# A new layout of the first stage: softmax passes of the first batch on VectorE, eight rooms for gated h, other slots for exp, slabs, w_out and loads

## The chip, the cores and the metric

The kernel runs on one core of one Trainium2 chip. The metric is the device time of one execution in microseconds, the median of three runs. All times below are microseconds unless marked ns. Engines are named as the profile names them: PE is TensorE's matmul stream and PEld its weight loads, DVE is VectorE, ACT is ScalarE, POOL is GpSimd, SP is SyncE, whose one queue issues every DMA of this kernel in program order.

## The reference, cut to what matters

Eight batches of eight heads with 576 tokens and head size 64 are reduced to 32 memory slots each, and the result goes through two gated feed-forward layers of 4608 tokens, width 512 and inner width 2048. The weights are handed in as 64-bit floats.

```python
a = exp(phi - phi.max(2)); a = a / (a.sum(2) + 1e-9)           # over tokens
k_m = einsum('bhsm,bhsd->bhmd', a, k)
v_m = einsum('bhsm,bhsd->bhmd', a, v)
s = (q @ k_m.T) / sqrt(64); s = exp(s - s.max(-1))
x = (s / (s.sum(-1) + 1e-9)) @ v_m                              # -> 4608 x 512
x = moe(x, w_in, w_out);  x = moe2(x, w_in2, w_out2)
# moe:  h = x @ w_in; g = h * sigmoid(1.702 h); g @ w_out
# moe2: the same with sigmoid(h)
```

## The kernel before, in words

**Stages.** Stage 1 (0 to about 380) is the attention of all batches and the first layer's w_in, up to the gated h, which goes to DRAM in `gs`. Stages 2, 3 and 4 (380 to 748, to 1110, to 1473) are the three other weight products; the change leaves their body alone and touches only the first few steps of stage 2. Every float32 product is made of three passes with a high and a low part of each operand, so each operand is rounded (a copy on ACT) and its rest is formed (a subtraction on DVE or POOL).

**Slots of stage 1.** A loop over 256 slots (L1003), 32 for each batch, sets the order. A slot is six matmuls of 128x288 (`first1`, L331) into one of four PSUM buffers `h`, and the gate, which ACT writes to `g` (L348, Silu). While exponentials are due nearby (the list `exps`, L827), the gate is a Tanh on ACT (L345) and one instruction on DVE (L346), which saves loads of ACT's function table. Two slots (two token halves `hf`) fill one `g` tile; there are five rooms for `g` (L342). `g_store` (L350) sends the tile to DRAM.

Ahead of its own gate a slot emits the operations that are listed for it with "e" (mostly evacuations and vector work), then come its matmuls and gate, then "p" (other matmuls), "l" (more evacuations), "d" (DMA issues). The table `PLAN` (L728) gives the slot of each operation for batch 1, for 2 and for 3 and later, counted from the start of the batch ahead. The first batch's order is written out in `start`, with the rest of it in `zero`.

**Attention of a batch.** phi is loaded, its maximum folded (`pm`, two halves on DVE, L172), subtracted, exponentiated (`phi_exp`, L201) and its sum folded (`es`, eight instructions on POOL, L175). `kv_mm` (L211, 72 matmuls) gives k_m and v_m. q is loaded in eight pieces, transposed on PE (`q_t`, L244) and copied out as `qT` (`q_e`, L248); `scores` (L256), a transposition on DVE (`soft_t`), maximum, subtraction (`soft_sub`, L282), exp (`soft_exp`, L286), sum, multiplication (`soft_mul`, L296), back transposition (`soft_back`, L300) and high and low part of the result (`soft_hi` L304, `soft3`) follow for each half. `wp_mm` multiplies v_m into w_in and gives a `slab` (ACT high L322, DVE low L326), four of them per batch; the slots' matmuls read slabs and attention output.

**Weights.** A 64-bit weight tile is converted in two ACT passes (L94, L95), a shift and a sign on DVE (L100, L105) and an addition on POOL (L111). The 16 tiles of w_in are converted in the first 25 slots. w_out is loaded in four groups of four tiles (`wo_load`, L394) through two rooms `raw` (L391), so that each load waits until the tile two before it is converted. Sums of these (`w_sums`) and their high and low parts (`w_high` L448, `w_low`) are spread over stage 1.

**Start of stage 2.** `r_fetch` (L495) reads `gs` back from slots given by `rf`, `a_prep` makes the operand tiles `op` (ACT L520, DVE L523); two of them are made in stage 1 at `mk`.

## Time and profile before

| | us |
|---|---|
| median of three runs | 1475.28 (1474.56 to 1476.45) |
| the profiled execution | 1474.05 |
| its span in the trace | 1472.3 |
| PE busy | 1396.1 (95%) |
| DVE busy | 963.1 (65%) |
| ACT busy | 812.2 (55%) |
| POOL busy | 207.0 (14%) |

The execution's own time holds 1.75 us outside the span; it lies 1.23 us under the median. PE is the engine with the most work in each stage. The page's rows by instruction group and the chain of waits show where it stood still; the windows by stage show in which part of the span.

### The profile page before, as it was taken

How to read it: one execution, taken by the hardware profiler on the slowest of the kernel's cores; microseconds unless marked ns; L12 is line 12 of the kernel's file. 1: busy time of each engine (PE TensorE's matmuls, PEld its weight loads, DVE VectorE, ACT ScalarE, POOL GpSimd, SP SyncE). 2: the span in 40 equal slices, each digit the busy share in tenths (PEclk: the TensorE clock that was granted, in tenths of full speed). 3: DMA queues.
4: the chain of work that ended last, by engine and by line, in shares of the span. 5: the costliest groups of instructions: out<-in, count | busy, mean ns of one | idle time of the engine just before them, and what ended most of it. 6: DMA issues, size and time to landing. Idle time of an engine off the chain costs nothing.

```text
span 1472.3 us, 27420 instructions
## 1 busy us (share of the span) xinstructions
PE 1396.1 (95%) x10776; PEld 1326.8 (90%) x10776; DVE 963.1 (65%) x1299; ACT 812.2 (55%) x1429; POOL 207.0 (14%) x193
## 2 busy tenths in 40 slices
PE   4789889999899999999999999999998999999998
PEld 3568677878899999999999999999998999999998
DVE  5745554544597898788877353454577776777765
ACT  3756766667455454455467565665674444444443
POOL 3423635432101111110000010111000000000000
PEclk9999999999999999999999999999999999999999
DMA  9777777945744836627234556465564524515320
GB/s 307 211 226 220 246 252 221 288 158 199 268 135 148 279 103 209 214 100 260 94 129 166 186 182 216 153 217 189 172 213 145 204 81 146 194 44 183 131 96 33
DMA packets 195296, 265.51 MB, mean 180 GB/s; under 512 B 50528, under 2 KB 158048, under 8 KB 195168
## 3 DMA queue, kind: packets, MB, share of 16 engines
q1 hardware_dynamic: 195168, 263.77, 53.9%
q8 instruction: 84, 1.38, 0.4%
q14 instruction: 44, 0.36, 0.1%
HBM read 159.91 MB, written 102.76 MB: 178 GB/s over the span
## 4 chain that ended last, share of the span: by engine, by line
PE 78%; DMA 7%; DVE 5%; ACT 3%; issue 1%; SPq 1%; POOL 0%; ACTq 0%; DVEq 0%
PE p L687 23%; PE p L537 17%; PE xb L625 13%; PE h L339 11%; PE y L625 10%; PE aa L256 2%; DMA xs<-o 1%; DMA rr<-gs 1%; DVE op L65 1%; PE a L211 1%; DMA q<-in_q_dram 1%; SPq L495 1%; DMA gs<-g 1%; PE a L244 1%; DVE r L62 1%
## 5 line engine op out<-in xcount | busy, mean ns | idle before, releaser
L537 PE MATMUL p<-op,wq 128*128 128x384 f32 x2016 | 358.4, 339 | 9.9 <-DVE op L65 4.5
L537 PEld LDWEIGHTS p<-op,wq 128*128 128x128 f32 x2016 | 353.0, 189 | 15.0 <-DVE op L65 7.7
L687 PE MATMUL p<-wq,op 128*128 128x256 f32 x3024 | 360.0, 282 | 4.2 <-ACT gq L635 2.5
L687 PEld LDWEIGHTS p<-wq,op 128*128 128x128 f32 x3024 | 359.6, 191 | 4.7 <-ACT gq L635 2.8
L520 ACT CAST op<-rr 128x768 fp32r<-128x768 f32 x216 | 179.2, 835 | 181.2 <-PE p L687 77.3
L339 PE MATMUL h<-attnT,slab 128*128 128x288 f32 x1536 | 239.2, 307 | 18.3 <-ACT g L348 14.0
L65 DVE TENSOR_TENSOR op<-rr,op 128x768 fp32r<-128x768 f32 x216 | 209.0, 974 | 66.2 <-ACT op L520 65.5
L339 PEld LDWEIGHTS h<-attnT,slab 128*128 128x128 f32 x1536 | 212.9, 193 | 41.6 <-ACT g L348 20.5
L625 PE MATMUL xb<-xq,wq 128*128 128x384 f32 x1152 | 216.4, 336 | 1.3 <-ACT e L665 0.9
L625 PEld LDWEIGHTS xb<-xq,wq 128*128 128x128 f32 x1152 | 201.4, 188 | 2.0 <-ACT e L665 1.2
L65 DVE TENSOR_TENSOR op<-r,op 128x768 fp32r<-128x768 f32 x120 | 123.2, 1031 | 73.8 <-ACT op L520 73.7
L625 PE MATMUL y<-xq,wq 128*128 128x384 f32 x864 | 166.6, 337 | 2.1 <-ACT e L675 1.0
L520 ACT CAST op<-r 128x768 fp32r<-128x768 f32 x120 | 99.4, 834 | 101.3 <-PE p L687 43.9
L625 PEld LDWEIGHTS y<-xq,wq 128*128 128x128 f32 x864 | 151.7, 188 | 3.0 <-ACT e L675 1.3
L348 ACT ACTIVATE g<-h 128x288 f32<-128x288 f32 x247 | 98.2, 420 | 77.2 <-PE h L339 59.4
L111 POOL TENSOR_TENSOR wst<-wst 128x512 int32<-128x512 int32 x24 | 40.9, 1704 | 488.4 <-DVE wst L105 279.5
L635 ACT ACTIVATE gq<-e 128x384 f32<-128x384 f32 x144 | 75.9, 527 | 28.7 <-DVE e L62 27.9
L62 DVE TENSOR_TENSOR e<-e,y 128x384 f32<-128x384 f32 x96 | 52.7, 552 | 47.4 <-PE y L625 45.5
L62 DVE TENSOR_TENSOR e<-e,xb 128x384 f32<-128x384 f32 x48 | 26.5, 553 | 84.0 <-PE xb L625 53.3
L65 DVE TENSOR_TENSOR slab<-aa,slab 128x512 fp32r<-128x512 f32 x62 | 39.8, 680 | 45.1 <-ACT slab L322 42.8
L448 ACT CAST wq<-wst 128x512 fp32r<-128x512 f32 x83 | 51.2, 620 | 25.1 <-DVE wst L65 15.0
L65 DVE TENSOR_TENSOR wq<-wst,wq 128x512 fp32r<-128x512 f32 x63 | 43.0, 687 | 13.4 <-ACT wq L448 13.3
(121 smaller groups left out, 1239.5 us busy)
## 6 DMA issues: line engine op xcount, KB each, us to landing
rr<-gs SPq DMA_DIRECT2D x120, 384.0 KB, 6.4
gs<-g SPq DMA_DIRECT2D x128, 288.0 KB, 4.0
gs<-gq SPq DMA_DIRECT2D x192, 192.0 KB, 1.9
r<-gs SPq DMA_DIRECT2D x72, 384.0 KB, 5.7
xs<-o SPq DMA_DIRECT2D x24, 384.0 KB, 3.6
xr<-xs SPq DMA_DIRECT2D x24, 384.0 KB, 4.4
out_dram<-o SPq DMA_DIRECT2D x24, 384.0 KB, 2.8
rawe<-in_moe_w_in_dram SPq DMA_DIRECT2D x16, 512.0 KB, 6.8
```

The lines of the kernel that those rows point to most:

```text
L62: eng.tensor_tensor(out=out, in0=a, in1=b, op=ALU.add)
L65: eng.tensor_tensor(out=out, in0=a, in1=b, op=ALU.subtract)
L111: nc.gpsimd.tensor_tensor(out=z, in0=z, in1=parts(t, dst)[0], op=ALU.add)
L256: nc.tensor.matmul(out=out[s][32 * j:32 * j + 32, 0:n], lhsT=st["kvT", b][r, i, 32 * j:32 * j + 32], rhs=rhs[j][r], start=True, stop=True)
L339: nc.tensor.matmul(out=h, lhsT=slab[b, f // 4, g][:, wi, f0:f0 + 128], rhs=x[:, g, xi], start=(g == 0 and n == 0), stop=(g == 1 and n == 2))
L348: nc.scalar.activation(out=t, in_=h, func=ACTF.Silu, scale=2.0)
L448: nc.scalar.copy(out=t[:, :, 0], in_=wst[m, c, k])
L520: nc.scalar.copy(out=t[:, :, 0], in_=s)
L537: nc.tensor.matmul(out=out[:, d, :HB], lhsT=w[:, s, wi, d * 128:(d + 1) * 128], rhs=t[:, s, gi], start=(start and p == 0 and s == 0 and n ...
L625: nc.tensor.matmul(out=out, lhsT=w[:, s, wi, f0:f0 + 128], rhs=x[:, s, xi], start=(start and s == 0 and n == 0), stop=(s == 1 and n == 2), ...
L635: nc.scalar.activation(out=t, in_=h, func=ACTF.Silu, scale=2.0)
L687: nc.tensor.matmul(out=out[:, d], lhsT=t[:, u, gi, d * 128:(d + 1) * 128], rhs=w[:, u, wi], start=(start and d != 1 and p == 0 and u == 0 ...
```

## The change

- `g` has eight rooms for five.
- `raw` is gone. The loads of the first three groups of w_out use two rooms of the pool that w_in's loads had used (`wo14`, `wo15`), in turn; the fourth group has one tile in the room of `kv`, with a place for each of its four loads.
- `es` can be folded on DVE in one instruction; it is so for batches 1 and 2, and on POOL for the later ones, at slot -7 for -14.
- In the first batch's softmax the multiplication of the first half and the subtraction of the second go from POOL to DVE. In the other batches `se` says which of the four subtractions and multiplications run on POOL (1 and -1) and which on DVE (0, -2): over the whole stage subtractions on POOL go from 4 to 9 and on DVE from 12 to 7.
- `qv` lets a copy of `qT` run on DVE (DVE 4 to 11 copies). `le` names the engine of the attention's low part (DVE 2 to 7, POOL 14 to 9). Some low parts and sums of w_out go to DVE (POOL 20 to 11 low parts).
- `ld` writes out the order of the first batch's loads, w_in and q mixed.
- The table has other slots in nearly every row. The exponentials' stretches begin one slot earlier in six batches; the list of them goes from (47,48), (79,80), ..., (175,176) to (46,48), (78,80), ..., (174,176). Gates by Tanh go from 9 to 14, Silu from 247 to 242; ACT loads its table 18 times in either.
- `rf` goes from [19, 20, 21, 22, 23, 2] to [20, 15, 22, 20, 27, 1], `mk` from [26, 29] to [21, 28]: the operand made first now stands one slot behind the issue of the fetch that it reads.

```diff
-            gt[b, f] = moe.tile([128, 2, HS], F32, tag="g", name="g", bufs=5)
+            gt[b, f] = moe.tile([128, 2, HS], F32, tag="g", name="g", bufs=8)
...
-            n = slice(2 * n, 2 * n + 2)
+            n = slice(2 * n, 2 * n + 2) if name == "pm" else slice(0, 4)
...
-    def raw():
-        return moe.tile([128, 512, 2], I32, tag="raw", name="raw", bufs=2)
...
-        st["wo", c, k] = wload(w1o, rows(f), cols(0), raw())
+        if c < 3:
+            t = wo_p.tile([128, 512, 2], I32, tag=f"wo{14 + k % 2}", name="raw")
+        else:
+            if k == 0:
+                t = att.tile([128, 2, 4, C9, D], F32, tag="kv", name="raw")
+                st["raw"] = t.rearrange("p a b c d -> p (a b c d)").bitcast(I32)
+            t = st["raw"][:, 1024 * k:1024 * k + 1024].rearrange("p (f w) -> p f w", w=2)
+        st["wo", c, k] = wload(w1o, rows(f), cols(0), t)
...
-                 'se': [0, 1, -2, 1]},
+                 'se': [1, 1, 0, 1],
+                 'ee': 1,
+                 'qv': [0, 0, 0, 0, 0, 0, 0, 1],
+                 'le': [0, 1]},
...
-             'wo': [[[53, 56, 62, 64], [62, 64, 65, 72], 73], [[101, 100, 105, 109], [108, 110, 114, 117], 121],
-                    [[151, 150, 157, 160], [156, 159, 165, 167], 173], [[216, 218, 222, 225], [222, 224, 227, 230], -3]],
+             'wo': [[[52, 54, 60, 61], [59, 61, 64, 69], 74], [[103, 97, 106, 109], [108, 109, 114, 117], 122],
+                    [[148, 147, 154, 157], [153, 156, 162, 166], 176], [[222, 224, 230, 232], [228, 231, 233, 236], 1]],
...
-        at(z + x["es"], "e", phi_fold, b, "es", ALU.add, nc.gpsimd)
+        at(z + x["es"], "e", phi_fold, b, "es", ALU.add, (nc.vector, nc.gpsimd)[x["ee"]])
...
-                at(z + y[9], "e", soft3, b, hf)
+                at(z + y[9], "e", soft3, b, hf, (nc.vector, nc.gpsimd)[x["le"][hf]])
```

On DVE, in the first batch's softmax (`sm` and `nat` are the sums and the scores of a half, `attnT` the low part of the result), the difference between the two orders is this:

```order
-L300 STREAM_TRANSPOSE at<-nat 128x576
-L274 STREAM_TRANSPOSE nat<-aa 128x288 x2
-L278 TENSOR_REDUCE mx<-nat 128x18
+L248 COPY qT<-a 128x288
+L296 TENSOR_TENSOR nat<-nat,sm 128x576
+L300 STREAM_TRANSPOSE at<-nat 128x576
+L274 STREAM_TRANSPOSE nat<-aa 128x288 x2
 L65 TENSOR_TENSOR attnT<-at,attnT 128x2x288
+L278 TENSOR_REDUCE mx<-nat 128x18
+L282 TENSOR_TENSOR nat<-nat,mx 128x576
```

The multiplication (L296) stands ahead of the back transposition and the subtraction (L282) ahead of what follows; both were on POOL, and one more copy of `qT` stands in front.

On ACT, ahead of the k_m and v_m matmuls of batch 2, where the second half of batch 1's scores is exponentiated and `qT` of batch 2 is copied; before:

```order
L286 ACTIVATE nat<-nat 128x576
L322 CAST slab<-aa 128x512 x2
L248 COPY qT<-a 128x288
L348 ACT_TABLE_LOAD
L348 ACTIVATE g<-h 128x288
L248 COPY qT<-a 128x288
```

and now:

```order
L201 ACTIVATE phi<-phi 128x576 x2
L345 ACTIVATE g<-h 128x288
L286 ACTIVATE nat<-nat 128x576
L248 COPY qT<-a 128x288 x2
L348 ACT_TABLE_LOAD
L348 ACTIVATE g<-h 128x288
L322 CAST slab<-aa 128x512
```

Both copies of `qT` now stand straight behind the exponential; the slab's two casts and the table load stand behind them.

On ACT, in the stretch of exponentials of batch 2's scores and batch 3's phi; before:

```order
L286 ACT_TABLE_LOAD
L286 ACTIVATE nat<-nat 128x576
L201 ACTIVATE phi<-phi 128x576
L345 ACTIVATE g<-h 128x288
L286 ACTIVATE nat<-nat 128x576
L201 ACTIVATE phi<-phi 128x576
L348 ACT_TABLE_LOAD
```

and now (L452 is a rounding of w_out, L448 in the numbering of before):

```order
L201 ACT_TABLE_LOAD
L201 ACTIVATE phi<-phi 128x576
L345 ACTIVATE g<-h 128x288
L286 ACTIVATE nat<-nat 128x576
L452 CAST wq<-wst 128x2x256
L345 ACTIVATE g<-h 128x288
L286 ACTIVATE nat<-nat 128x576
L201 ACTIVATE phi<-phi 128x576
L348 ACT_TABLE_LOAD
```

The same four exponentials and two table loads now hold two gates instead of one, and a rounding of w_out stands among them.

On POOL, around the additions that end the conversion of the first four w_out tiles (L111; `es` is batch 3's fold, `attnT` the low part of a result); before:

```order
L175 TENSOR_TENSOR es<-phi 128x128
L175 TENSOR_TENSOR es<-es,phi 128x128 x7
L65 TENSOR_TENSOR attnT<-at,attnT 128x2x288 x2
L111 TENSOR_TENSOR wst<-wst,raw 128x2x256 x4
L65 TENSOR_TENSOR wst<-wst 128x512 x2
```

and now:

```order
L175 TENSOR_TENSOR es<-phi 128x128
L175 TENSOR_TENSOR es<-es,phi 128x128 x7
L65 TENSOR_TENSOR attnT<-at,attnT 128x2x288
L111 TENSOR_TENSOR wst<-wst,raw 128x2x256 x2
L65 TENSOR_TENSOR attnT<-at,attnT 128x2x288
L111 TENSOR_TENSOR wst<-wst,raw 128x2x256 x2
L65 TENSOR_TENSOR wst<-wst 128x512 x2
```

The first two additions have moved up ahead of the second low part. The plan puts them at slots 59 and 61 for 62 and 64, and the fold at slot 57 for 50.

## Rows read from the trace of the kernel before

**Rows 1.** Windows by stage: length; busy PE, PEld, DVE, ACT, POOL; PEclk; DMA; GB/s.

```profile
0.00:380.00 380.00, 325.67 (x3720) 263.91 (x3721) 198.93 (x351) 246.26 (x539) 151.43 (x161) 0.97 0.74 235
380.00:748.00 368.00, 358.11 (x2017) 352.95 (x2017) 309.98 (x352) 183.18 (x244) 29.80 (x16) 0.99 0.51 172
```

**Rows 2.** The same by stretch of the first stage and the start of the second.

```profile
60.00:105.00 45.00, 34.93 (x540) 26.19 (x541) 25.67 (x46) 26.29 (x55) 18.99 (x25) 0.96 0.68 197
...
200.00:260.00 60.00, 52.56 (x581) 43.97 (x580) 32.22 (x59) 43.25 (x93) 31.71 (x33) 0.97 0.70 226
...
380.00:415.00 35.00, 29.32 (x144) 27.58 (x144) 22.83 (x28) 13.46 (x20) 0.00 (x0) 0.90 0.52 188
```

**Rows 3.** The same of two stretches at half clock.

```profile
216.40:219.80 3.40, 3.40 (x15) 3.40 (x15) 2.71 (x5) 3.35 (x8) 3.17 (x5) 0.51 1.04 407
...
404.20:407.60 3.40, 3.40 (x13) 3.40 (x12) 2.41 (x3) 0.83 (x1) 0.00 (x0) 0.50 0.00 0
```

**Rows 4.** Timeline of TensorE: start, duration, operation, count, idle time before it and releaser.

```profile
79.88 1.79 PE L339 MATMUL h<-attnT,slab 128*128 128x288 f32 x6
...
96.58 0.40 PE L211 MATMUL a<-kv,phi 64*32 64x128 f32 x2 [1.30 <-ACT qT L248]
...
98.59 2.31 PE L211 MATMUL a<-kv,phi 64*32 64x128 f32 x142 [1.61 <-ACT qT L248]
...
144.47 3.41 PE L339 MATMUL h<-attnT,slab 128*128 128x288 f32 x24
...
150.35 1.09 PE L339 MATMUL h<-attnT,slab 128*128 128x288 f32 x6 [2.47 <-ACT g L348]
...
171.54 3.50 PE L339 MATMUL h<-attnT,slab 128*128 128x288 f32 x24 [1.10 <-ACT g L348]
...
202.38 0.44 PE L244 MATMUL a<-ident,q 96*128 96x96 f32 x3 [1.66 <-DMA q<-in_q_dram]
...
216.21 4.18 PE L339 MATMUL h<-attnT,slab 128*128 128x288 f32 x18 [3.31 <-ACT g L348]
...
299.26 3.46 PE L339 MATMUL h<-attnT,slab 128*128 128x288 f32 x24 [1.33 <-ACT g L348]
...
356.21 1.68 PE L339 MATMUL h<-attnT,slab 128*128 128x288 f32 x6 [1.84 <-ACT g L348]
...
403.80 4.27 PE L537 MATMUL p<-op,wq 128*128 128x384 f32 x14 [2.81 <-ACT o L549]
```

**Rows 5.** Timeline of ScalarE, same columns, around four of these waits.

```profile
94.58 0.69 ACT L286 ACTIVATE nat<-nat 128x576 f32<-128x576 f32 x1 [2.40 <-POOL nat L282]
...
96.55 1.28 ACT L348 ACT_TABLE_LOAD   x1
...
148.78 0.66 ACT L94 ACTIVATE wst<-raw 128x512 f32<-128x512 f32 x1 [2.98 <-DMA raw<-in_moe_w_out_dram]
...
214.46 1.28 ACT L348 ACT_TABLE_LOAD   x1 [2.00 <-DMA gs<-g]
...
382.61 0.71 ACT L348 ACTIVATE g<-h 128x288 f32<-128x288 f32 x2 [3.21 <-DMA gs<-g]
```

**Rows 6.** Timelines of VectorE and GpSimd: a multiplication, a subtraction, an evacuation.

```profile
37.21 0.76 DVE L296 TENSOR_TENSOR nat<-nat,sm 128x576 f32<-128x576 f32 x1
...
93.58 1.58 DVE L296 TENSOR_TENSOR nat<-nat,sm 128x576 f32<-128x576 f32 x1
...
97.33 0.63 DVE L65 TENSOR_TENSOR slab<-aa,slab 128x512 fp32r<-128x512 f32 x1
...
93.39 1.16 POOL L282 TENSOR_TENSOR nat<-nat,mx 128x576 f32<-128x576 f32 x1 [7.09 <-DVE mx L278]
```

**Rows 7.** Groups of stage 1 by form: count | busy, mean ns | idle before, releasers.

```profile
L172 DVE TENSOR_REDUCE pm<-phi 128x64 f32<-128x576 f32 x16 | 18.4, 1172 | 9.5 <-DMA phi<-in_phi_dram 9.4
...
L65 DVE TENSOR_TENSOR attnT<-at,attnT 128x576 fp32r<-128x576 f32 x2 | 1.5, 752 | 0.7 <-ACT attnT L304 0.7
...
L65 POOL TENSOR_TENSOR attnT<-at,attnT 128x576 fp32r<-128x576 f32 x14 | 20.0, 1430 | 15.5 <-ACT attnT L304 15.5
```

More of the change, by code (lines that the diff above doesn't have):

```diff
@@ L106, in wsign, with wadd, wconv1 @@
                                            op0=ALU.bitwise_and, op1=ALU.bitwise_or)
-    def wadd(t, dst):
+    def wadd(t, dst, eng):
         if t.dtype == I32:
             z = dst.bitcast(I32)
-            nc.gpsimd.tensor_tensor(out=z, in0=z, in1=parts(t, dst)[0], op=ALU.add)
-    def wconv1(t, dst):
+            eng.tensor_tensor(out=z, in0=z, in1=parts(t, dst)[0], op=ALU.add)
+    def wconv1(t, dst, eng):
         wshift(t, dst)
         wsign(t, dst)
-        wadd(t, dst)
+        wadd(t, dst, eng)
     def psa():
@@ L473, in w2_conv1 @@
     def w2_conv1(m, n):
-        wconv1(st.pop(("c2", m, n)), st["c2s", m, n])
+        wconv1(st.pop(("c2", m, n)), st["c2s", m, n], nc.gpsimd)
     def w2_store(m, n):
@@ L724, in evac @@
             o_store(b, 1, 0, t)
-    PLAN = {1: {'phi': [0, 2],
-                 'kv': [4, 5, 6, 7, 8, 9, 9, 10],
+    PLAN = {1: {'phi': [1, 3],
+                 'kv': [2, 3, 4, 5, 6, 7, 7, 8],
                  'pm': [4, 6],
-                 'mt': 9,
-                 'mr': 10,
-                 'mb': 10,
+                 'mt': 6,
+                 'mr': 7,
+                 'mb': 7,
                  'sb': [12, 12],
@@ L740, in attn_moe_moe @@
                  'ke': 19,
[3 rows of a table removed]
-                 'soft': [[21, 22, 22, 22, 24, 26, 27, 28, 29, 29], [24, 25, 26, 26, 27, 28, 29, 30, 32, 32]],
-                 'se': [1, 0, 1, 0]},
[3 rows of a table added]
+                 'soft': [[21, 22, 22, 22, 24, 26, 27, 28, 29, 29], [24, 25, 25, 26, 27, 28, 29, 30, 33, 33]],
+                 'se': [-1, 0, 1, 1],
+                 'ee': 0,
+                 'qv': [1, 0, 0, 0, 0, 3, 0, 0],
+                 'le': [1, 1]},
              2: {'phi': [-18, -16],
@@ L752, in attn_moe_moe @@
                  'sb': [-8, -7],
-                 'ex': [-8, -6],
-                 'es': -4,
+                 'ex': [-6, -6],
+                 'es': -5,
                  'mm': -3,
@@ L757, in attn_moe_moe @@
                  'kt': 0,
[4 rows of a table removed]
-                 'soft': [[5, 6, 7, 9, 15, 17, 18, 20, 21, 24], [11, 12, 13, 14, 16, 18, 20, 25, 26, 26]],
-                 'se': [0, 0, 1, 0]},
-             3: {'phi': [-29, -28],
-                 'kv': [-35, -32, -29, -26, -23, -21, -14, -14],
-                 'pm': [-25, -25],
[4 rows of a table added]
+                 'soft': [[5, 6, 7, 9, 15, 20, 21, 23, 24, 27], [11, 12, 13, 14, 16, 21, 24, 29, 31, 31]],
+                 'se': [-1, 0, 1, 0],
+                 'ee': 0,
+                 'qv': [0, 0, 0, 0, 0, 0, 0, 0],
+                 'le': [1, 1]},
+             3: {'phi': [-31, -30],
+                 'kv': [-34, -31, -25, -25, -22, -21, -13, -13],
+                 'pm': [-26, -24],
                  'mt': -22,
@@ L770, in attn_moe_moe @@
                  'sb': [-19, -18],
-                 'ex': [-17, -16],
-                 'es': -14,
+                 'ex': [-18, -16],
+                 'es': -7,
                  'mm': -4,
-                 'norm': -2,
+                 'norm': -1,
                  'kt': 0,
[4 rows of a table removed]
-                 'soft': [[5, 6, 7, 8, 15, 17, 18, 19, 20, 23], [11, 12, 13, 14, 16, 18, 20, 24, 29, 30]],
[14 rows of a table removed]
-                       ('wl', 0, 0), ('wh', 0, 1), ('wl', 0, 1), ('exp', 1), ('sum', 1), ('mul', 1, 0), ('back', 1),
[12 rows of a table removed]
[4 rows of a table added]
+                 'soft': [[5, 6, 7, 11, 15, 16, 18, 19, 20, 23], [11, 12, 13, 14, 16, 18, 20, 23, 26, 26]],
[17 rows of a table added]
+                       ('wh', 0, 1), ('wl', 0, 0), ('exp', 1), ('wl', 0, 1), ('sum', 1), ('mul', 1, 0), ('back', 1),
[9 rows of a table added]
                       [16, 'e', ('c0', 2, 3), ('c0', 3, 3)],
                       [16, 'l', ('sh', 2, 3), ('sh', 3, 3), ('sg', 3, 3), ('sg', 2, 3), ('ad', 2, 3)], [19, 'p', ('wp', 3)],
[6 rows of a table removed]
[7 rows of a table added]
              'gap': 8,
@@ L898, in w1_conv0 @@
         wconv0(st["w1", kk, j], w1[:, kk, cols(j)])
-    w1_load(0, 0, 0)
-    w1_load(1, 1, 0)
-    for n in range(2):
-        for i in range(2):
-            load_kv0(i, n)
-    for p in range(4):
-        load_q(0, 0, p)
-    w1_load(2, 2, 0)
-    w1_load(3, 3, 0)
-    for p in range(4):
-        load_q(0, 1, p)
-    for j in (1, 2):
-        for kk in range(4):
-            w1_load(4 * j + kk, kk, j)
+    for o in PLAN["ld"]:
+        if o[0] == "w":
+            w1_load(4 * o[2] + o[1], o[1], o[2])
+        elif o[0] == "k":
+            load_kv0(o[1], o[2])
+        else:
+            load_q(0, o[1], o[2])
     vec, pool = nc.vector, nc.gpsimd
```

14 lines of the change are left out of this document (5 added, 9 removed), and 86 rows, old and new, of the table PLAN.

## The prediction

> **What bounds the kernel now.** I read the windows by stage first. PE is busy 325.67 of the first 380 us and 358.11 of the next 368 [rows 1]: stage 1 has 54 us of idle PE, a stage that the change does not touch about 10. No other engine is near full in stage 1 (DVE 198.93, ACT 246.26, POOL 151.43) [rows 1], so what costs there is not an engine's amount of work but the order in which PE's suppliers deliver. Next came the timeline of PE, where each row names what ended the idle time ahead of it [rows 4], and for each large wait the timeline of the engine named [rows 5]. The reader is to see three kinds of wait: a gate `g` that ACT could not write because it was held by something else, a `qT` copy, and a transfer. Third are the windows' clock columns. Around 216 and 404 PE was granted 0.51 and 0.50 of its speed for 3.4 us [rows 3], its lower level of 1.2 GHz, behind waits of 3.31 and 2.81 [rows 4]. There a slot of six matmuls takes 1.79, where 24 matmuls (four slots) take 3.41 [rows 4], 0.85 a slot: a stretch of 3.4 us at half clock does the work of half of it and costs about 1.7. So a wait that is followed by such a stretch is worth itself and 1.7.
>
> **The change part by part.** All sums are made against the profiled execution's 1474.05 us, of which 1.75 lie outside its span; it is 1.23 under the median.
>
> First batch. The multiplication goes from POOL to DVE: 0.76 for some 1.16 [rows 6], and so does a subtraction; 2 x 0.4 = 0.8 comes off the chain to the first slabs, a further `qT` copy ahead of it on DVE costs part of that. I take -0.6, between -1.2 (two handoffs fall away as well) and +1.2 (one operation's worth of new queueing on DVE).
>
> k_m and v_m of batch 2. PE waits 1.30 and 1.61 for two `qT` copies [rows 4]. Ahead of them ACT waited 2.40 for POOL's subtraction, and after that did the exponential, the slab casts and a table load of 1.28 [rows 5]. By the order both copies now stand right behind the exponential. What is late next is that exponential itself, whose subtraction stays on POOL. I take -2.3 of the 2.91. `es` of this batch, now on DVE, costs two halves like `pm`'s, 2 x 1.17 = 2.3 [rows 7], in a stretch where DVE is 57% busy [rows 2]; it is hidden behind the slots, but if it lands ahead of a slab's low part it takes these 2.3 back. So -2.9 to 0.
>
> First w_out group. PE waits 2.47 at 150.35 [rows 4], because ACT at 148.78 waited 2.98 for the third `raw` tile [rows 5], whose load waits until the first tile is converted. The first conversion moves from slot 62 to 59, the third from 65 to 64: two slots of 0.85 more room, 1.7 of the 2.98, and the four `h` buffers cover what is left. The wait and a half-clock stretch behind it (2.47 + 1.7 = 4.2) go for the most part; POOL's fold now stands just ahead of the addition that frees the room. I take -3.5, from -4.2 to 0.
>
> Exponentials. Three stretches end in a wait for a gate of 1.10 to 1.33 (171.54 the first, 299.26 the last) [rows 4]. By the order the same exponentials and the same two loads now hold one more gate and, in the first of them, a rounding as well. ACT's extra work is the same and PE gets one more slot's product done meanwhile, which counts only where ACT was idle in that slot. I take -0.5 for two of the three and nothing for the one with the rounding: -1.0, from -3.5 (all three gone) to +1.
>
> q. The wait of 1.66 for a load of q at 202.38 [rows 4] goes, as the transposition that frees its room stands three slots earlier: -1.5, from -1.7 to 0.
>
> Eight rooms for `g`. At 214.46 ACT's table load waited 2.00 until a store freed a room [rows 5], since SP was held by a load of w_out that waited for its room; PE then waited 3.31 at 216.21 and ran at half clock [rows 3, 4]. Three more rooms are six more slots, about 5 us, more than the 2.00. The rest of the 3.31 is the stretch of exponentials and stays. 2.0 + 1.7 and 0.3 for the second of SP's waits gives -4.0, from -5 to 0.
>
> Fourth w_out group. The wait of 1.84 at 356.21 [rows 4] comes from the two rooms; with four places no load waits for a conversion. With the half clock behind it -3.5, from -3.5 to -1.5.
>
> Into stage 2. ACT waits 3.21 at 382.61 for a room of `g` [rows 5], and 2.81 at 403.80 [rows 4] stand in a stretch with PE busy 29.32 of 35 at a clock of 0.90 [rows 2], with the half-clock stretch of [rows 3] in it. Eight rooms remove the first; the operands come from the same transfers. I take -3, from -7 (the 5.7 idle and part of the clock) to +1.
>
> Sum of the gains: -0.6 - 2.3 - 3.5 - 1.0 - 1.5 - 4.0 - 3.5 - 3.0 = -19.4.
>
> New waits. DVE gets five low parts of results (0.75 each for 1.43 on POOL [rows 7]); they stand in batches 3 to 7 ahead of slab parts, and I take half of 5 x 0.75 as on the path: +1.9. The first operand of stage 2 is made one slot behind its fetch, so ACT waits there with gates behind it; four `h` buffers cover 3.4 us of it: +1.0 (0 to 3). The low part of batch 1's second half is wanted sooner: +0.75. Of the five new subtractions on POOL, see below, +1.0. One half-clock stretch behind a new wait: +1.7. Together +6.35.
>
> Subtractions on POOL. A DVE multiplication took 1.58 beside POOL's subtraction of 1.16 (93.58, 93.39) and 0.76 alone [rows 6]; a slab's low part at 97.33, which reads one operand from PSUM, took 0.63 [rows 6] while POOL was still folding. Five such subtractions cost between 0 and 5 x 0.82 = 4.1; I take 1.0, one collision and something, because in the new places slab parts stand beside them. The Trainium skill ("SBUF — State Buffer", section "Who interferes with whom") says that DVE and GpSimd share a port pair under an exclusive lock, which DVE needs for two SBUF inputs but not for one, and never for a tensor_reduce: by it the trace's pair of rows agrees, and the five would cost what stands beside them with two SBUF inputs, at most the 4.1, which makes the sum 1464.
>
> -19.4 + 6.35 = -13.05: 1474.05 - 13.05 = **1461.0**.
>
> **The rivals.** *All gaps close and nothing new comes*: 1474.05 - 19.4 = 1454.7, and 1446 with the lower ends of the largest terms (transition -4, exponentials -2.5, batch 2 and w_out -1.3 more). For it speaks that ACT, DVE and POOL are all far from full [rows 1]; against it that each row of the table moves, so that waits which nobody has seen appear. Chance 0.20.
>
> *The gaps change hands*: ACT's queue in front of the gates is as long as before, and half of the sum is given back by new waits of a gate; 1474.05 - 9.7 + 6.35 = 1470.7. The rounding among the exponentials and the early operand speak for it. Chance 0.17. *The rooms bring nothing*, as SP still stands at a load of w_out (its third of the second group is issued at slot 106 and waits for a conversion at 108): then 4.0 stays, 1465; this lies within my forecast's own case. *Given back entirely*, within the 0.2% (2.95 us) about the median that a measurement of this kernel can tell from no change: 1472.3 to 1478.2, chance 0.12.
>
> *Slower: DVE's queue.* DVE works in order, and the change gives it some 18 us more (two folds of 2.3, five low parts of 0.75, seven copies, low parts and sums of w_out, five more gates' second halves). If in batches 1 to 7 a slab's low part, on which the slots' matmuls wait, is late by 3.0 and a half-clock stretch of 1.7 follows, that is 7 x 4.7 = 32.9, against 19.4 of gains: 1474.05 + 13.5 = 1487.6. It decides from 19.4 / 7 = 2.8 a batch. Against it: DVE is busy 25.67 of 45 and 32.22 of 60 us in two stretches [rows 2], and none of the waits in [rows 4] names DVE as what ended it. Chance 0.09.
>
> **How the numbers follow.** My forecast's case (1455 to 1467) has 0.42, all closing 0.20, changing hands 0.17: faster by over 0.2% 0.79, within it 0.12, slower 0.09. The range reaches down to 1449, leaving some 0.07 below, and up to 1475, leaving a third of the even case and the slower one, 0.13, above. The forecast is given as 1461.
>
> **What would show it.** In the trace after: windows of the first 380 us with PE still at 325 busy, but stage 2 starting some 10 us sooner; no wait of ACT's table load for a store of `g`; no wait of ACT's conversions for `raw`; k_m and v_m of batch 2 without a wait for `qT`; fewer stretches at a clock of 0.5 than before. It is wrong if the slots show new waits for slab parts or for DVE's half of the gate, if a stretch of exponentials with three Tanh gates ends in a longer wait than 1.3, or if ACT stands at the first operand of stage 2 for more than 4 us.

## The result and the profile after

The changed kernel takes 1456.29 us (median of four, 1455.83 to 1458.38) against 1475.87 of before beside it: ratio 0.9871, interval 0.9854 to 0.9888, 19.6 us less. In a later session the same program took 1458.82 (six executions, 1455.04 to 1463.70) against 1474.99: 0.9897, 0.9874 to 0.9919, 16.2 less. The forecast was 1461, a gain of 13; the range held the time. The sign and the mechanism (waits in stage 1 go, those that come are fewer) were right. The sum was a fifth to a third too small, and several of its terms were right only in total.

The profiled execution has a span of 1454.5, 17.8 less than before. The windows by stage (the columns of [rows 1]), cut at 365 us, 3 us ahead of the first w_out product, are:

```profile
0.00:365.00 365.00, 319.50 (x3696) 259.32 (x3697) 213.99 (x376) 242.30 (x527) 125.88 (x132) 0.97 0.77 244
365.00:733.00 368.00, 359.85 (x2049) 354.11 (x2047) 311.20 (x354) 186.91 (x253) 29.48 (x16) 1.00 0.51 173
```

Up to the first w_out product (380.08 us before, 368.27 now) idle PE falls from 54.3 to 45.5 us. In the first window DVE rises from 198.93 to 213.99 [rows 1], POOL falls from 151.43 to 125.88, and in the second window PE is busy 1.7 more. The start of each slot in both traces shows where the 17.8 came from; the table is worked out from the first matmul of the slot (minus is earlier than before):

| slot | start before | start after | difference |
|---|---|---|---|
| 0 | 33.45 | 36.66 | +3.2 |
| 8 | 51.33 | 54.60 | +3.3 |
| 16 | 70.06 | 70.28 | +0.2 |
| 32 | 102.93 | 99.66 | -3.3 |
| 40 | 112.56 | 111.61 | -1.0 |
| 64 | 142.37 | 140.16 | -2.2 |
| 72 | 157.29 | 149.09 | -8.2 |
| 80 | 165.90 | 158.70 | -7.2 |
| 112 | 207.97 | 199.61 | -8.4 |
| 120 | 222.38 | 211.22 | -11.2 |
| 224 | 347.44 | 335.47 | -12.0 |
| 232 | 359.71 | 343.02 | -16.7 |
| 248 | 373.73 | 358.15 | -15.6 |
| first of stage 2 | 380.08 | 368.27 | -11.8 |
| after its 168th matmul | 419.64 | 401.89 | -17.8 |
| end | 1472.27 | 1454.48 | -17.8 |

So the first batch is later in this profile, not earlier. Slots 16 to 32 gain 3.5, of which 2.3 are lost again by slot 40. Three steps (slots 64 to 72, 112 to 120, 224 to 232) give 13.5, and the slots behind the first and the last of them take back 1.0 and 1.1. The end of stage 1 loses 3.8 and the start of stage 2 gives back 5.9. From there on nothing changes. Among the waits of PE that remain, these are the ones that the text below speaks of (columns of [rows 4]):

```profile
36.66 0.85 PE L339 MATMUL h<-attnT,slab 128*128 128x288 f32 x2 [0.67 <-ACT slab L322]
...
50.77 1.05 PE L256 MATMUL aa<-w,kvT 64*32 64x512 f32 x4 [2.00 <-POOL w L111]
...
97.75 0.96 PE L339 MATMUL h<-attnT,slab 128*128 128x288 f32 x6 [0.73 <-ACT g L348]
101.78 0.40 PE L339 MATMUL h<-attnT,slab 128*128 128x288 f32 x1 [0.84 <-ACT attnT L304]
103.26 3.34 PE L339 MATMUL h<-attnT,slab 128*128 128x288 f32 x23 [1.08 <-POOL attnT L65]
125.15 3.44 PE L339 MATMUL h<-attnT,slab 128*128 128x288 f32 x24 [0.53 <-ACT g L348]
164.34 3.47 PE L339 MATMUL h<-attnT,slab 128*128 128x288 f32 x24 [0.68 <-ACT g L348]
...
202.66 1.06 PE L339 MATMUL h<-attnT,slab 128*128 128x288 f32 x6 [1.29 <-DVE g L346]
...
361.03 7.40 PE L339 MATMUL h<-attnT,slab 128*128 128x288 f32 x42 [1.90 <-ACT g L348]
386.30 3.93 PE L541 MATMUL p<-op,wq 128*128 128x384 f32 x21 [1.90 <-DVE wq L65]
```

The waits of [rows 4] at 96.58 and 98.59 (`qT` of batch 2), 150.35 (w_out), 202.38 (q), 216.21 (room of g) and 356.21 (`raw`) have no row left in this trace. New are three in a row at 97.75 to 103.26 and the one at 361.03, and two that DVE ends: its half of a gate at 202.66, in the stretch where the 3.31 was, and a part of a weight at 386.30.

To compare many profiles I add up, from such rows, all waits of PE in slots 16 to 255 that have an engine or a transfer as their releaser ("waits" in the table of runs below): 23.3 before, 13.2 after. By engine that is 15.5 and 6.2 for ACT, 5.1 and 5.9 for DVE, 0.3 and 1.1 for POOL, 2.4 and 0 for transfers. Two other things differ between two executions of the same program, and are left out of that sum: waits that the trace calls "issue", and where PE runs at half clock.

### The profile page after: what moved, and what is told of

Same layout as the page of the kernel before. It is cut to its first block, busy times and chain, and to the rows that moved or that the text cites. A ratio compares the mean times of both kernels' runs of the same rounds, so it can differ in the third digit from the quotient of the medians.

```text
span 1454.5 us, 27408 instructions
## 1 busy us (share of the span) xinstructions
PE 1391.3 (96%) x10776; PEld 1323.6 (91%) x10776; DVE 979.1 (67%) x1326; ACT 810.5 (56%) x1422; POOL 181.1 (12%) x164
## 4 chain that ended last, share of the span: by engine, by line
PE 78%; DVE 7%; ACT 5%; DMA 5%; issue 3%; SPq 2%; POOL 0%; ACTq 0%; DVEq 0%
PE p L691 25%; PE p L541 14%; PE xb L629 13%; PE h L339 11%; PE y L629 10%; DVE op L65 2%; PE aa L256 2%; DMA rr<-gs 1%; PE a L211 1%; DVE r L62 1%; DMA wst<-in_moe_w_in_dram 1%; DMA raw<-in_moe_w_out_dram 1%; PE a L244 1%; ACT g L348 1%; SPq L162 1%
## 5 line engine op out<-in xcount | busy, mean ns | idle before, releaser
L339 PE MATMUL h<-attnT,slab 128*128 128x288 f32 x1536 | 236.2, 306 | 11.9 <-ACT g L348 4.6
L111 POOL TENSOR_TENSOR wst<-wst 128x512 int32<-128x512 int32 x24 | 40.6, 1691 | 486.5 <-DVE wst L105 286.3
L452 ACT CAST wq<-wst 128x512 fp32r<-128x512 f32 x83 | 51.1, 618 | 25.1 <-DVE wst L65 15.5
L65 DVE TENSOR_TENSOR wq<-wst,wq 128x512 fp32r<-128x512 f32 x72 | 49.6, 692 | 17.0 <-ACT wq L452 16.9
```

Of the source, the lines that this page charges most:

```text
L65: eng.tensor_tensor(out=out, in0=a, in1=b, op=ALU.subtract)
L111: eng.tensor_tensor(out=z, in0=z, in1=parts(t, dst)[0], op=ALU.add)
L339: nc.tensor.matmul(out=h, lhsT=slab[b, f // 4, g][:, wi, f0:f0 + 128], rhs=x[:, g, xi], start=(g == 0 and n == 0), stop=(g == 1 and n == 2))
L452: nc.scalar.copy(out=t[:, :, 0], in_=wst[m, c, k])
```

## The experiments

The runs were made in three sessions, each beside its own executions of before (medians 1476.67, 1474.99 and 1475.76). Executions of one program lay up to 13 us apart there, so the ratios carry intervals of 0.002 to 0.004, 3 to 6 us. What a part is worth under that is read from single waits in the trace and from the time that PE takes for a stretch of slots. Sums of waits between 12.1 and 15.3 are hardly told apart, since the two profiles of the changed kernel itself have 13.2 and 14.5. The stretches repeat better: slots 40 to 64, 64 to 80, 96 to 112, 112 to 120 and 224 to 248 take 28.6 to 28.8, 18.5 to 19.1, 18.5 to 18.6, 11.4 to 11.6 and 22.7 us in every profile of the new order whose edit leaves them alone. Before they took 29.8, 23.5, 20.4, 14.4 and 26.3, so some 14 us of the gain stand in these five, each time (three of before's stretches at half clock, 5.1 us, are among them).

| run | median | ratio to before (interval) | waits, slots 16 to 255 |
|---|---|---|---|
| before | 1475.87 | 1 | 23.3 |
| changed | 1456.29 | 0.9871 (0.9854 to 0.9888) | 13.2 |
| changed, again | 1458.82 | 0.9897 (0.9874 to 0.9919) | 14.5 |
| new order, old rooms | 1460.92 | 0.9894 (0.9874 to 0.9915) | 14.1 |
| old order, new rooms | 1468.33 | 0.9950 (0.9921 to 0.9978) | 22.7 |
| five rooms for g | 1463.96 | 0.9899 (0.9868 to 0.9931) | 12.1 |
| first batch's two passes on POOL | 1455.96 | 0.9859 (0.9819 to 0.9898) | 14.3 |
| q load earlier | 1460.31 | 0.9899 (0.9874 to 0.9925) | 12.4 |
| first operand later | 1459.84 | 0.9903 (0.9878 to 0.9929) | 13.3 |
| low part on DVE | 1457.89 | 0.9884 (0.9864 to 0.9905) | 11.0 |
| w_out's first group as before | 1464.09 | 0.9925 (0.9899 to 0.9951) | 15.1 |
| phi's sum on POOL | 1457.16 | 0.9882 (0.9858 to 0.9907) | 14.1 |
| first exponential later | 1460.62 | 0.9902 (0.9878 to 0.9925) | 15.3 |
| three mends | 1451.46 | 0.9846 (0.9821 to 0.9872) | 11.3 |

### The changed kernel again

No edit.

> The changed kernel once more, as the yardstick of the runs beside it and of what differs between two executions of the same program. Theory: waits that come from the order (a gate, a copy, a slab part) stand in the trace at the same places with the same size within 0.2 us: in slots 16 to 255 13 us in sum as in the profile after, 27 before slot 16, 3 at the start of stage 2. What differs are the waits that the trace calls issue (4.4 in the profile after, 10.0 with five rooms) and the stretches at half clock. Rival: the order's waits themselves wander by several us, and then single profiles can't tell parts of the change apart. Time 1454 to 1460.

1458.82. The order's waits stand where they stood: 1.05, 0.84 and 1.09 at slots 31 to 33 (0.73, 0.84, 1.08 above), 0.55 and 0.71 for 0.53 and 0.68, 1.96 at slot 249 for 1.90. Others moved by more than the 0.2 of the theory (2.39 for 1.36 at slot 20, 0.95 for 1.29 at slot 114), and those before slot 16 were 29.3 for 27.3, since the first batch hangs on transfers. So the theory holds for the places from slot 16 on and, in sum, to 1.3 us; ahead of slot 16 it does not hold. The clock's stretches moved. Windows of the changed kernel in its first profile (first two rows) and in this one (last two; columns of [rows 1]):

```profile
0.00:45.00 45.00, 21.69 (x255) 15.15 (x256) 25.44 (x51) 17.65 (x32) 9.50 (x19) 0.81 0.99 286
45.00:120.00 75.00, 63.83 (x779) 47.88 (x779) 51.91 (x83) 49.23 (x104) 24.44 (x19) 1.00 0.76 232
```

```profile
0.00:45.00 45.00, 19.77 (x249) 14.06 (x249) 24.58 (x50) 16.76 (x30) 9.38 (x18) 0.89 0.98 286
45.00:120.00 75.00, 62.56 (x727) 46.51 (x728) 48.48 (x78) 46.12 (x98) 23.36 (x18) 0.93 0.69 211
```

The granted clock was 0.81 in the first 45 us and full in the next 75 in one, 0.89 and 0.93 in the other. From slot 16 to 120 this second execution lost 3.6 us against the first, and after slot 120 nothing. It has two stretches of 3.4 us at a clock of 0.50 there, from 83.9 and from 107.8, and the first execution has none; at 1.7 each they are nearly all of the 3.6.

### New order, old rooms; old order, new rooms

```diff
-            gt[b, f] = moe.tile([128, 2, HS], F32, tag="g", name="g", bufs=8)
+            gt[b, f] = moe.tile([128, 2, HS], F32, tag="g", name="g", bufs=5)
...
-        if c < 3:
-            t = wo_p.tile([128, 512, 2], I32, tag=f"wo{14 + k % 2}", name="raw")
-        else:
...
+        t = moe.tile([128, 512, 2], I32, tag="raw", name="raw", bufs=2)
```

> The new order with the old rooms: five rooms for g, two rooms raw for all loads of w_out. Theory: the gain of 19.6 us is the sum of an order part and a rooms part. In the profile after, PE gained 2.8 to 5 us around slots 114 to 120 (room of g and the half clock behind it) and 4.7 around slots 231 and 232 (two raw rooms), so without the new rooms 7 to 9 us are lost: 1463 to 1466. Rival one, the rooms bring nothing because the new order alone moves the loads far enough: 1456 to 1458. Rival two, the order needs the rooms and without them its loads hold the DMA queue: 1470 or more.

The second takes the kernel before, puts eight rooms and the new places for `raw` into it, and moves the fourth w_out group behind the use of `kv`:

```diff
-                    [[151, 150, 157, 160], [156, 159, 165, 167], 173], [[216, 218, 222, 225], [222, 224, 227, 230], -3]],
+                    [[151, 150, 157, 160], [156, 159, 165, 167], 173], [[222, 222, 224, 225], [226, 227, 228, 230], -3]],
```

> The order before with the new rooms: eight for g, wo14 and wo15 for three groups of w_out, four places in the room of kv for the fourth, whose loads go to slots 222 to 225 and conversions to 226 to 230 because the room is taken until 220. Theory: the rooms part alone, 5 to 9 us: 1467 to 1471. Rival one (the rooms bring nothing): 1475 to 1477. Rival two (rooms and order only pay together): 1474 or more as well, but with the g wait at slot 116 gone from the trace and another wait in its place.

The order alone gave 15.7 us (1460.92 against 1476.67), the rooms alone 8.3 (1468.33 against 1476.67). The two add up to 24.1, more than the 19.6 or 16.2 of both together. With intervals of 3 and 4 us on the two that alone says little; that they remove some of the same waits is seen in the rows. The order alone came out 2 better than expected, the rooms alone as expected.

With the old order and the new rooms, PE at the stretch of exponentials that had waited 3.31 [rows 4] and at the w_out conversion:

```profile
149.62 1.06 PE L339 MATMUL h<-attnT,slab 128*128 128x288 f32 x6 [2.19 <-ACT g L348]
...
215.17 2.81 PE L339 MATMUL h<-attnT,slab 128*128 128x288 f32 x18 [1.32 <-ACT g L348]
```

The rooms take 2.0 off the 3.31 and leave 1.32, the exponentials' own part, as the prediction had it; the w_out wait stays at 2.19. With the new order and the old rooms, five of them for `g`, the 3.31 is gone as well: from slot 112 to 120 that profile gained 3.0 against before, the rooms alone and the changed kernel 2.8 each. So either is enough there. What the order did is seen on SP, which stood at a load of w_out until POOL's addition freed the room. Its waits from 190 to 212 us (total, times, longest), before and with the new order and the old rooms:

```profile
SPq L77 <- POOL wst L111: 8.5, 2, 8.3
```

```profile
SPq L77 <- POOL wst L111: 4.9, 2, 4.1
```

SP stands half as long, the stores of `g` behind it leave sooner, and ACT's wait for a room is 0.18 us for 2.00. The start of stage 2 goes with the order too: from its first matmul to after its 168th it takes 39.6 us before, 38.8 with the rooms alone, 33.9 with the order alone and 33.6 in the changed kernel. Where the new order does need the rooms is the fourth w_out group. New order, old rooms, ACT and PE:

```profile
352.95 0.66 ACT L94 ACTIVATE wos<-raw 128x512 f32<-128x512 f32 x1 [1.72 <-DMA raw<-in_moe_w_out_dram]
...
356.97 0.66 ACT L94 ACTIVATE wos<-raw 128x512 f32<-128x512 f32 x1 [1.91 <-DMA raw<-in_moe_w_out_dram]
```

```profile
354.52 2.68 PE L339 MATMUL h<-attnT,slab 128*128 128x288 f32 x18 [1.10 <-ACT g L348]
358.54 2.68 PE L339 MATMUL h<-attnT,slab 128*128 128x288 f32 x18 [1.34 <-ACT g L348]
```

Two conversions wait for two loads, and PE for two gates behind them, 2.44 us; the changed kernel has no such row.

### Five rooms for g

```diff
-            gt[b, f] = moe.tile([128, 2, HS], F32, tag="g", name="g", bufs=8)
+            gt[b, f] = moe.tile([128, 2, HS], F32, tag="g", name="g", bufs=5)
```

> The changed kernel with five rooms for g and nothing else undone. Theory: the wait of ACT for a room of g returns at the stretch of exponentials near slot 112 (2.0 us, with a half-clock stretch of 1.7 behind it) and at the start of stage 2 (up to 3): 1459 to 1463. Rival: the new order sends the stores in time, eight rooms hold nothing up: 1456 to 1457, no wait for a store of g in the trace.

1463.96 is 1 us above the theory's range, but its ratio of 0.9899 is not to be told from the changed kernel's 0.9871 and 0.9897. The waits table of its first 440 us (total, times, longest) has

```profile
ACT g L348 <- DMA gs<-g: 2.4, 3, 1.3
```

against waits of 2.00 and 3.21 before [rows 5]; none of the three ends in a wait of PE at an exponential, and PE's waits sum to 12.1. The theory's wait did not return. That eight rooms for g are worth anything under the new order was not shown.

### The first batch's two passes back on POOL, and the q load earlier

```diff
-('mul', 0, 0)
+('mul', 0, 1)
...
-('sub', 1, 0)
+('sub', 1, 1)
```

> The changed kernel with the first batch's multiplication (first half) and subtraction (second half) back on POOL. Theory A (the prediction's): DVE is 0.4 us quicker for each, so the first slot starts up to 0.8 later than 36.66. Theory B: in the changed kernel the multiplication stands on DVE behind a copy of qT that waits 1.96 us for a late load of q; on POOL it starts right after the sum, so the first slot starts 1 to 1.5 earlier, at about 35.3. In both, slot 8 waits for the w_in additions on POOL, which are the same work plus 2.3 us ahead of them, so the end time moves by -1 to +1: 1455 to 1457.5.

```diff
-('w', 3, 0), ('q', 1, 2), ('w', 3, 1), ('w', 0, 2), ('w', 0, 1), ('q', 1, 3),
+('w', 3, 0), ('q', 1, 2), ('q', 1, 3), ('w', 3, 1), ('w', 0, 2), ('w', 0, 1),
```

> The changed kernel with the last of the first batch's q loads issued three w_in loads earlier. Theory: the multiplication of the first half stands on DVE behind a copy of qT that waited 1.96 us for this load; with the load earlier the wait is gone, the first slot starts 1.5 to 2.3 us earlier (34.4 to 35.2 for 36.66) and so does the second half. Whether this reaches the end: slots 7 and 8 wait for w_in additions on POOL (2.0 at 50.77). Theory A: these start from the same loads and do not move, so slot 8 stays at 54.6 and the time is the same within 1 us. Theory B: their conversions stand behind the softmax on ACT and DVE and come earlier with it, so slot 8 and the end gain 1.5 to 2.

In the changed kernel DVE has its sums at 30.65 and multiplies at 32.98, because a copy of `qT` stands in front that waits for PE, and PE for a load of q:

```profile
31.86 0.71 PE L244 MATMUL a<-ident,qe 96*128 96x96 f32 x3 [2.22 <-DMA qe<-in_q_dram]
```

```profile
32.61 0.46 DVE L248 COPY qT<-a 128x288 f32<-128x288 f32 x1 [1.96 <-PE a L244]
32.98 0.75 DVE L296 TENSOR_TENSOR nat<-nat,sm 128x576 f32<-128x576 f32 x1
33.77 0.78 DVE L300 STREAM_TRANSPOSE at<-nat 128x576 f32<-128x576 f32 x1
```

With the multiplication on POOL it runs at once, and the wait only moves one instruction on, to the back transposition, which is DVE's anyway (POOL, then DVE):

```profile
30.28 1.16 POOL L296 TENSOR_TENSOR nat<-nat,sm 128x576 f32<-128x576 f32 x1 [0.48 <-DVE sm L292]
```

```profile
32.53 0.46 DVE L248 COPY qT<-a 128x288 f32<-128x288 f32 x1 [2.39 <-PE a L244]
32.90 0.77 DVE L300 STREAM_TRANSPOSE at<-nat 128x576 f32<-128x576 f32 x1
```

Slot 0 starts at 36.37 for 36.66 and 37.35 in the two profiles of the changed kernel. Seven more runs leave this part as it is; in all nine profiles the copy waits 0.70 to 3.40 us and slot 0 starts at 33.84 to 37.80, so the edit shows no gain. Theory B named the right wait and not what stands behind it: from the end of the copy to slot 0 it takes 3.4 us with POOL and 3.2 to 3.6 in the nine. The time, 1455.96 (1450.76 to 1463.56), shows no loss by POOL. With the load earlier the copy waits no more:

```profile
30.56 0.39 DVE L248 COPY qT<-a 128x288 f32<-128x288 f32 x1
30.87 0.74 DVE L296 TENSOR_TENSOR nat<-nat,sm 128x576 f32<-128x576 f32 x1
31.65 0.78 DVE L300 STREAM_TRANSPOSE at<-nat 128x576 f32<-128x576 f32 x1
```

Slot 0 starts at 33.73, and at 33.38 in the run with three mends, which has the same edit: ahead of all nine that have the load late. That the load order makes the copy wait is shown. How much it delays slot 0 depends on when the load lands, 29.25 to 32.85 in the nine, so a single profile does not size it. Further on nothing is shown: slot 8 starts at 53.49 and 53.17 with the load early and at 52.12 to 57.02 in the nine, slot 16 at 67.56 and 66.88 for 67.90 to 72.68. PE waits 2.0 for POOL's w_in addition ahead of slot 7 in every one of these profiles, so they do not decide between theories A and B. In the median nothing shows (1460.31 against 1458.82, ratios 0.9899 and 0.9897).

### The first operand of stage 2 later

```diff
-             'mk': [21, 28],
+             'mk': [25, 28],
```

> The changed kernel with the first operand of stage 2 made four slots later (slot 249 for 245). Theory: ACT's wait of 1.70 for the fetch, with the gates of four slots behind it, goes; so do PE's 1.90 at slot 249 and the half-clock stretch behind it, 3.7 us in all at slot 255; the start of stage 2 keeps at least two of them, since its first matmuls need the operand only 7 slots later: the end gains 2 to 3.7. Rival: stage 2's start is bound by fetches and by DVE, and gives it all back: slot 255 earlier by 3, end the same within 0.5.

In the changed kernel ACT stood at this operand:

```profile
359.84 0.83 ACT L524 CAST op<-r 128x768 fp32r<-128x768 f32 x1 [1.70 <-DMA r<-gs]
```

With the edit PE's wait at slot 249 and the half clock behind it are gone: from slot 248 to the first matmul of stage 2 it took 6.4 us, for 10.1 in both profiles of the changed kernel. Six other runs with the operand in its early place have a wait of 1.4 to 2.0 at slot 249 without a half-clock stretch behind it, and take 8.1 to 8.7. Then it is given back. PE and ACT in stage 2:

```profile
377.83 0.44 PE L541 MATMUL p<-op,wq 128*128 128x384 f32 x1 [2.20 <-ACT op L524]
```

```profile
376.95 0.83 ACT L524 CAST op<-rr 128x768 fp32r<-128x768 f32 x1 [5.03 <-DMA gs<-g]
```

The third operand waits for transfers that the edit does not make earlier; PE arrives sooner and waits. By the 168th matmul 2.0 of 3.7 us were left against the first profile, 1.0 against the second, and the time (1459.84) shows none: the rival.

### The low part on DVE

```diff
-[24, 25, 25, 26, 27, 28, 29, 30, 33, 33]
+[24, 25, 25, 26, 27, 28, 29, 30, 32, 32]
...
-                 'le': [1, 1]},
+                 'le': [1, 0]},
```

> The changed kernel with batch 1's second half of the attention output one slot earlier and its low part on DVE for POOL. Theory: the waits of PE for the high part (0.84) and the low part on POOL (1.08) at slot 33 go or shrink to under 0.5, every later slot starts 1.5 to 2 earlier, and since nothing between slot 34 and the end of stage 1 waits for anything that the DMA queue decides alone, the end gains 1.5 to 2. Together with the q load (no gain in its time) and the later first operand (none either) this should be what the three mends in one gained; but those gained 7, so a gain here of 5 to 7 is the rival: one wait less also takes a stretch at half clock away.

The rows for 0.84 and 1.08 are gone and no other took their place: slots 32 to 40 take 2.5 us less than in the changed kernel, and the waits fall to 11.0. The time, 1457.89 (0.9884), is as expected or no gain; the interval of the ratio holds both. In its profile 2.72 and 3.62 us of "issue" waits stood at two other places and took the gain back; up to stage 2 these waits came to 8.4 us, for 4.4 in the first profile of the changed kernel.

### The first w_out group at its slots of before

```diff
-             'wo': [[[52, 54, 60, 61], [59, 61, 64, 69], 74],
+             'wo': [[[53, 56, 62, 64], [62, 64, 65, 72], 74],
```

> The changed kernel with the first w_out group's loads and conversions at their slots of before (53, 56, 62, 64 and 62, 64, 65, 72). Theory: the third load again waits for the first conversion until slot 65 or 66, ACT waits some 3 us for it, and PE 2 to 2.5 for a gate at slot 69, where before had 2.47; with or without a stretch at half clock behind it 2 to 4.5 us in the end. Rival: in the new order another engine frees the room sooner, the wait is under 1.

```profile
149.47 0.67 ACT L94 ACTIVATE wst<-raw 128x512 f32<-128x512 f32 x1 [2.53 <-DMA raw<-in_moe_w_out_dram]
```

```profile
147.00 2.55 PE L339 MATMUL h<-attnT,slab 128*128 128x288 f32 x17 [1.06 <-POOL attnT L65]
...
151.06 1.06 PE L339 MATMUL h<-attnT,slab 128*128 128x288 f32 x6 [0.44 <-ACT g L348]
152.68 0.72 PE L256 MATMUL aa<-qT,kvT 64*32 64x288 f32 x16 [0.55 <-DVE slab L65]
```

ACT again waits 2.53 for the third load (0.41 in the changed kernel), but of that only 0.44 reaches PE as a wait for a gate at slot 69, where the theory had 2 to 2.5. A new wait joins it: on POOL an addition stands in front of a low part for which PE waits 1.06. From slot 56 to 80 it lost 3.3 us, with PE at full clock there. 1464.09, ratio 0.9925, is the slowest of the variants of the changed kernel, with an interval that overlaps theirs. That the old slots cost what the theory says is shown by the stretch; that they do it through the one wait is not.

### Phi's sum on POOL, and the first exponential later

```diff
-                 'ee': 0,
+                 'ee': 1,
```

(in batches 1 and 2)

> The changed kernel with the sum over phi of batches 1 and 2 back on POOL. Theory A: the fold on DVE (2.26 in the profile after) was free, and on POOL (4.1) it stands among the w_in additions of batch 0, so slots 13 to 24 wait 1 to 3 us more. Theory B, the prediction's slower rival: DVE's queue pays for the fold; without it the slabs and the second half's result of batch 1 come up to 2.3 earlier, and the waits at slots 31 to 34 (0.73, 0.84, 1.08) shrink by 1 to 2.

1457.16. Neither happened: the waits at slots 31 to 33 are 1.02, 0.84 and 1.09, as in the second profile of the changed kernel, and slots 13 to 24 did not get slower in step. The fold costs 2.26 on DVE and more on POOL, and PE waits for it on neither.

```diff
-                 'ex': [-18, -16],
+                 'ex': [-17, -16],
```

> The changed kernel with phi's first exponential of batches 3 to 7 one slot later, as before, so that the stretches of exponentials hold one Tanh gate less. Theory (the prediction's): PE's wait at the end of a stretch grows by 0.5 each, from 0.5 and 0.7 at 125 and 164 us to the 1.1 of before, and for five stretches by 2 to 2.5 in the end. Rival: the stretches stay as they are within 0.2, since ACT's work in them is the same.

```profile
125.13 3.48 PE L339 MATMUL h<-attnT,slab 128*128 128x288 f32 x24 [1.09 <-ACT g L348]
164.91 3.44 PE L339 MATMUL h<-attnT,slab 128*128 128x288 f32 x24 [1.33 <-ACT g L348]
204.29 3.57 PE L339 MATMUL h<-attnT,slab 128*128 128x288 f32 x24 [1.17 <-ACT g L348]
...
247.98 3.44 PE L339 MATMUL h<-attnT,slab 128*128 128x288 f32 x24 [1.10 <-ACT g L348]
...
287.38 3.45 PE L339 MATMUL h<-attnT,slab 128*128 128x288 f32 x24 [1.10 <-ACT g L348]
```

The five waits are 1.09 to 1.33, 5.8 in sum. In the changed kernel the five stretches have 0.53, 0.68, 1.29 and 0.63 (the last two behind DVE's half of a gate) and none over 0.3: 3.1. One more Tanh gate in the stretch is worth 2.7 in all, a little more than expected, and 0.5 on the mean, from nothing in the third stretch to about 1 in the fifth; the median (1460.62, 0.9902) goes that way without telling it apart.

### Three mends

The q load earlier, the first operand later and the low part on DVE together.

> Three mends in one: the q load earlier, the first operand of stage 2 four slots later, and in batch 1 the second half's high and low part one slot earlier with the low part on DVE. Theory: gains of 0 to 2 at slot 8, 1.9 near slot 33 (waits of 0.84 for the high and 1.08 for the low part), and 2 to 3.7 at slot 249, together 4 to 7 us against the changed kernel beside it: 1450 to 1453. Rival: waits move to what stands behind (slabs at slot 40, fetches of stage 2), 1455 to 1457.

1451.46 (1446.63 to 1456.32), ratio 0.9846, 0.9821 to 0.9872, the fastest of all. Against the changed kernel beside it (1458.82) it is 7.4 us less, a bit more than expected. One part of it is shown: slots 32 to 40 take 9.5 us, as with the low part on DVE alone, for 12.0 and 13.3 in the changed kernel. Slot 16 is 3.4 us earlier than in the first profile of the changed kernel, but only 1.0 ahead of the earliest of the nine above, so that may be luck. The later operand gives nothing here: PE waits at stage 2, now 3.42 us in one piece, and from slot 248 to after the 168th matmul of stage 2 it takes 42.8 us, for 43.7 and 42.7 in the changed kernel:

```profile
367.69 0.69 PE L541 MATMUL p<-op,wq 128*128 128x384 f32 x1 [3.42 <-ACT op L524]
```

The three single runs gained nothing, nothing and at most 2 in their medians, so the 7.4 is more than their sum, and the intervals (0.9846 ends at 0.9872, 0.9897 begins at 0.9874) only just part. Whether the mends help each other or this program's executions fell well is open.

## Why the prediction came out as it did

**First batch: -0.6, measured +3.2 at slot 0 and +0.2 at slot 16. Failed.** The step that failed is "a further `qT` copy ahead of it on DVE costs part of that". I priced the copy by its duration and not by what it waits for. The table `ld` had moved its load of q behind three loads of w_in, which I read as an order of loads and did not follow to the copy; it waited 1.96 us on DVE with the whole softmax behind it. Making the load earlier removed that, moving the multiplication to POOL did not. The sizes are of one execution: in the nine profiles with the late load slot 0 is 0.4 to 4.4 us later than before's 33.45, and slot 16 between 2.2 earlier and 2.6 later, so no gain shows, and at slot 16 no loss.

**k_m and v_m of batch 2: -2.3. The wait went, the gain did not stay.** The 2.91 of [rows 4] are gone. In their place 1.92 appeared at slot 33, at the result of batch 1's second half, which the new order puts one slot later, and 0.73 at slot 31 for a gate. I had 0.75 for that result among the new waits. From slot 16 to 40 PE takes 41.3 and 45.1 us in the two profiles of the changed kernel (no stretch at half clock and two) and 42.5 before (one). The run with the low part on DVE shows that the 1.92 was a matter of one slot and one engine.

**First w_out group: -3.5, measured -6.0 from slot 64 to 72,** of which the next eight slots take back 1.0. Mechanism right, undersized: the waits of 2.47 and 0.53 and the half clock (1.7) are 4.7 of the 5.0. The run with the old slots brings ACT's 2.53 back and loses 3.3 us there, though not by that wait alone.

**Exponentials: -1.0, measured -2.7 over five stretches.** The argument was right on the mean, 0.5, and I counted two of five. The stretch with the rounding is the one that ends at 164.34; the listing of ACT under "The change" shows that one, batch 3's scores and batch 4's phi, and not batch 2's scores and batch 3's phi as it says. It has 0.68, for 1.10 before and 1.33 with one gate less, so it gained like the others.

**q: -1.5.** The wait of 1.66 is gone; between slots 96 and 112 1.9 us are gained, in every profile of the new order.

**Eight rooms: -4.0, measured -2.8 from slot 112 to 120. Right for the old order, not needed in the new one.** The rooms alone do take 2.0 of PE's wait and 2.8 of the stretch. But the new order with five rooms gains the same 3.0 there. What the term had wrong is that it takes rooms to remove the wait: in the new order SP stands at the load of w_out for 4.1 us and not 8.3, and five rooms last that long.

**Fourth w_out group: -3.5, measured -4.7 from slot 224 to 232,** of which the next slots gave back 1.1, so -3.6. Here the places are needed and enough: the rooms alone take slots 224 to 248 from 26.3 to 22.7 us as well, and the new order with two rooms (2.44 of waits back) takes 25.7.

**Into stage 2: -3, and +1.0 for the early operand: measured -2.2 in sum.** The early operand cost 3.8 in the first profile: 1.90 at slot 249, within its 0 to 3, and the half clock behind it, which was the sum's one stretch of 1.7. In six runs without that stretch it cost 1.7 to 2.3. In the first 168 matmuls of stage 2 5.9 came back, and the step that was to give it, "Eight rooms remove the first", failed: the rooms alone do remove ACT's 3.21 and gain 0.7, the order alone with five rooms 5.7. Which of its slots does it was not tried. The run with the operand later shows that the two places hang together: PE meets the fetches sooner or later.

**DVE's queue, the slower rival.** There is 15 us more work on DVE in stage 1 [rows 1], and two of the prediction's signs of being wrong came: waits for DVE's half of the gate, 1.29 and 0.63, and one of 0.82 for a slab part at slot 119. But they stand where ACT's larger waits stood or are small, and all of PE's waits for DVE in slots 16 to 255 go from 5.1 to 5.9 only. The fold, the queue's largest piece, is free on either engine. The new waits were 6.35 in the sum; those listed (2.65 at slots 31 to 33, 1.29, and 3.8 at slot 249) come to 7.7, of which I had placed 3.45 rightly (0.75, 1.0 and the 1.7). Two of its terms did not come. For +1.9 by low parts on DVE, PE's waits for DVE's parts in batches 3 to 7 are 1.2 us and were 1.1. For +1.0 by subtractions on POOL, the DVE instructions beside all nine of them took 0.3 us longer in sum than their like elsewhere.

**What made the total larger** than -13 are these two terms, 2.9, the w_out group and the exponentials, and the clock. From slot 16 to the 168th matmul of stage 2 before has six stretches at half clock, 1.7 us each; the first profile of the changed kernel has one and the second three. The second one's span is 12.6 us shorter than before's, close to the forecast, and the first one's 17.8: where the clock fell is 3.4 of the difference, and that part is luck. Against the medians of before the gain is 16.2 to 19.6. One sum of the prediction is off without effect: the lower end of the first rival is 1446.9 by its own terms, not 1446.

## What to carry to other kernels

An instruction that is moved to an in-order engine brings along the wait of whatever now stands in front of it: price the neighbour by what it waits for, back to the load, not by its duration. Two edits that remove the same wait are worth it once, so run each alone before crediting it. Where PE waits further on for transfers that an edit does not make earlier, time saved in front of them is mostly given back there (here all but 1 to 2 of 3.7 us). Compare a place with every profile whose edit leaves it alone: slot 0 differed by 4 us between nine of them, slots 96 to 112 by 0.1.
